# Two kinds of stores put later in the SP queue of a Fourier filter and squared-ReLU network

## The chip, the cores and the metric

The kernel runs on one core of a Trainium2 chip. A core has a matrix engine (TensorE, "PE" in the profile), VectorE ("DVE"), ScalarE ("ACT"), GpSimd ("POOL") and SyncE ("SP"), which here only issues transfers. Each engine takes its own instructions in program order and waits on semaphores for the others. Sixteen DMA engines move the data of all queues. The metric is the device time of one launch in microseconds (us); lower is better.

## The reference

`x` has 8 batches of 3008 positions by 256 features. Each feature is filtered in the frequency domain along the positions; the result goes, row by row, through a network with a squared ReLU.

```python
X = np.fft.rfft(x, axis=1)                       # x: (8, 3008, 256)
y = np.fft.irfft(X * (filt_r + 1j * filt_i)[None], n=3008, axis=1)
h = np.maximum(y.reshape(24064, 256) @ w_in, 0)  # w_in: (256, 2048)
out = (h * h) @ w_out                            # w_out: (2048, 256)
```

Inputs and the output are float32.

## The kernel before, in words

**The transform.** 3008 is 64 times 47, and the filter is done as four rounds of small matrix products, in float16, with two trips through memory to turn the layout. For batch `b`:

- `load_x` (L186, on GpSimd's queue) brings a piece of `x` in, `unit_a` (L333, four for a batch) does the 47-point part. ScalarE (L354, L362) and VectorE (L356) copy the sums from `psA` to a tile `u`, of which there are three, and `write_u` (L326, called at the end of `unit_a`, L363) stores it with two transfers on SP's queue to `dU` in memory.
- `read_u` (L403) brings the whole batch back from `dU` in the other layout (`ut`, one buffer), with two transfers, 1.5 MB together. `unit_b` (L410, twelve a batch) does the 64-point part and multiplies by the filter on VectorE (L424); GpSimd's queue adds two halves (L431). `unit_p` (L454, twelve) goes back; ScalarE copies (L463) to `ze`, and after each third `unit_p` SP stores a block to `dZ` (L466). These are the four blocks `dZ`(b,0) to `dZ`(b,3).
- `read_z` (L475, four a batch, two transfers each, at L479) brings `dZ` back as `zt`, in one of two buffers. Every `read_z` reads from the results of all four blocks. `unit_y` (L483, sixteen) does the last part: PE at L497, copies at L504 and L506 to `yt`, the network's input.

**The network.** It runs in 47 groups of 512 rows. The main loop (L805) goes through slots, eight for each group. In slot `s`, `ffn_g1` (L511) computes two of sixteen blocks of the hidden layer into `psH`, of which there are two buffers; ScalarE applies the ReLU (L531), VectorE squares (L538). The second product of the group before runs in the same slots. Groups 0 to 45 do it with seven block products in place of eight (`products`, L629): VectorE builds sums of blocks (`sums`), PE multiplies (L640), and the output is put together in two tiles, `top` and `bot`, from three output buffers (`p_out`, L148). For group `g`, ScalarE starts `top` (L647) in slot 8g+9 and `bot` (L652) in slot 8g+13; `bot` is complete in slot 8g+15 (L657) and stored at once (L658); `top` is complete in slot 8g+16 (L661, on VectorE) and stored at once (L662). `store` (L561) uses one transfer (L578) or two or three pieces (L580), since rows are kept in a permuted order. The last group, 46, uses the plain product (L547) and `ffn_out` (L550), which stores tiles named `ost`.

**The order.** The transform of batch `b` is spread by hand over the slots before its rows are wanted. `fft_plan` (L666) gives every unit a time in slots, finds a free half slot near it, and puts the moves (`load_x`, `read_u`, `read_z`) at fixed half slots. The loop calls `run(work, s, 0)` after the first product of a slot and `run(work, s, 1)` after the second. So the order of all instructions of each engine is written out by this loop, SP's transfers too: SP takes them in that order and waits, at each, for what it needs.

Of the kernel before, what the change touches and what calls it, by code (L numbers as in the profile page):

```python
# [20 lines left out]
SLOTS = 8  # L21
# [89 lines left out]
def kernel(  # L111
# [214 lines left out]
    def write_u(b, c):  # L326
        u = us.pop((b, c))
        v = dU[b].rearrange("(m q) d -> q m d", q=48)
        for j in range(2):
            m = 16 * c + 8 * j  # L330
            nc.sync.dma_start(out=v[:, m:m + 8, :], in_=u[64 * j:64 * j + 48])

    def unit_a(b, c):  # L333

        pool, tag = (p_y, "yt") if (b, c) == (1, 3) else (p_u, "u")
        u = us[(b, c)] = pool.tile([112, 8, D], F16, tag=tag, name=f"u_{b}_{c}")
        ph = psH(f"psA_{b}_{c}")
        if b == 1 and c % 2:
            ps = [psO(f"psA_{b}_{c}_{h}").rearrange("p a d -> p (a d)") for h in range(2)]
        else:  # L340
            ps = [psF(f"psA_{b}_{c}_{h}") for h in range(2)]
        for i in range(2):
            for j in range(2):
                m = slice(4 * j + 2 * i, 4 * j + 2 * i + 2)
                for h in range(2):
                    p = slice(64 * h, 64 * h + N2)
                    o = ps[h] if i == 0 else ph[:, h, :]
                    nc.tensor.matmul(o[64 * j:64 * j + 64, :], sSA[p], x16s[(b, c)][p, m, :],  # L348
                                     start=True, stop=True)
        for h in range(2):  # L350
            o = u[:, h:h + 3:2, :]
            pv = ps[h][0:112, :].rearrange("p (e d) -> p e d", d=D)
            if h == 0 or b == 1:
                nc.scalar.copy(out=o, in_=pv)  # L354
            else:
                nc.vector.tensor_copy(out=o, in_=pv)  # L356
        o = u[:, 4:8, :].rearrange("p (e h) d -> p h e d", h=2)
        pv = ph[0:112].rearrange("p h (e d) -> p h e d", d=D)
        if b == 1:
            nc.vector.tensor_copy(out=o, in_=pv)  # L360
        else:
            nc.scalar.copy(out=o, in_=pv)  # L362
        write_u(b, c)  # L363

    def chunk_a0(c):

# [166 lines left out]
    def ffn_sq(g, s):  # L533
        n = 1 if g == NG - 1 else 2
        if (s + 1) % n:
            return
        v = h2s[g][:, 2 * (s + 1 - n):2 * s + 2, :]
        nc.vector.tensor_mul(out=v, in0=v, in1=v)  # L538
# [87 lines left out]
             ((6, 8, 16), (5, 8, 14)), ((5, 14, 16), (7, 0, 16)), ((2, 12, 16), (4, 0, 8)),  # L626
             ((4, 8, 16), (3, 0, 4)), ((3, 4, 16),))

    def products(g, k):  # L629

        f = sg[g]
        for p, m0, m1 in PARTS[k]:
            if p == 1 and m0 == 0:
                f["x"] = psO(f"psX_{g}").rearrange("p a (t c) -> p a t c", t=2)
            if p == 2 and m0 == 0:
                f["y"] = psO(f"psY_{g}").rearrange("p a (t c) -> p a t c", t=2)
            o = f["x"][:, 0] if p in (1, 6, 7, 4) else f["y"][:, 0 if p == 2 else 1]
            for m in range(m0, m1):
                q, t = divmod(m, 2)
                nc.tensor.matmul(o[:, t, :], f[p][:, q, 128 * t:128 * t + 128], sg["w"][p][:, q, :],  # L640
                                 start=(m == 0 and p in (1, 2)), stop=(q == 7),
                                 skip_group_check=True)
            if m1 < 16:
                continue
            if p == 1:
                f["top"] = p_out.tile([128, 2, 256], F32, tag="ost", name=f"top_{g}")
                nc.scalar.copy(out=f["top"][:, :, 0:128], in_=o)  # L647
            elif p == 6:
                nc.scalar.copy(out=f["top"][:, :, 128:256], in_=o)
            elif p == 7:  # L650
                f["bot"] = p_out.tile([128, 2, 256], F32, tag="ost", name=f"bot_{g}")
                nc.scalar.copy(out=f["bot"][:, :, 128:256], in_=o)  # L652
            elif p == 2:
                for v, i in ((f["top"][:, :, 0:128], 0), (f["bot"][:, :, 128:256], 1)):
                    nc.vector.tensor_add(out=v, in0=f["y"][:, i], in1=v)  # L655
            elif p == 4:
                nc.scalar.copy(out=f["bot"][:, :, 0:128], in_=o)  # L657
                store(g, 2, 2, f["bot"])  # L658
            elif p == 3:
                v = f["top"][:, :, 128:256]  # L660
                nc.vector.tensor_add(out=v, in0=o, in1=v)  # L661
                store(g, 0, 2, f["top"])  # L662

    YN = (45, 45.5, 46, 46.5, 48, 49.5, 51, 52.5, 54, 56, 58, 60, 63, 66, 69, 72)

    def fft_plan():  # L666

        fixed, units, moves = [], [], []
        for b in range(1, B):
            f = (b * S // TG) * SLOTS - (48 if b > 1 else 40)  # L670
            d = 0
            if b == 1:
                for n in range(4, 16):
                    fixed.append(((n if n < 8 else n + 2 if n < 12 else 2 * n - 7) + n % 2 / 2,
                                  unit_y, 0, n))
                moves.append((7.5, read_z, 0, 3))
                moves.append((0, read_u, b))
                d = 7
            else:
                for a in range(16):  # L680
                    if a % 2 == 0 and b > 2:
                        moves.append((f + ((-57 + 2.3 * a) if b == 3 else (-66 + 2.75 * a)),
                                      load_x, b, a // 2))
                    if a % 4 == 3:
                        units.append((f + ((-13, -9, -5.5, -3)[a // 4], -46 + 2.1 * a, -56 + 2.75 * a)[min(b, 4) - 2],
                                      unit_a, b, a // 4))
                moves.append((f + (2 if b == 2 else -6.5), read_u, b))
            for p in range(12):
                r = 12 + 16.5 * p / 11 if b == 1 else 6 + 28 * p / 11 if b == 2 else -2 + 36 * p / 11
                units.append((f + r, unit_b, b, p))  # L690
                if b == 1 and 2 <= p < 10:
                    moves.append((f + r, load_x, 2, p - 2))
                units.append((f + r + (4.5 if b == 1 else 7 - 2.5 * p / 11), unit_p, b, p))
            for c in range(4):
                moves.append((f + (40 + d / 14, 43, 48, 54)[c] - d, read_z, b, c))
            for n in range(16):
                (fixed if n < 4 else units).append((f + YN[n] - d, unit_y, b, n))
        work, used, done = {}, set(), {}
        for r, *u in fixed:
            h = int(2 * r)  # L700
            used.add(h)
            work.setdefault(h, []).append(u)
        rank = (unit_a, unit_b, unit_p, unit_y)
        for r, *u in sorted(units, key=lambda u: (rank.index(u[1]), u[0])):
            after = done.get((u[0], u[1]), -1)
            if u[0] is unit_a:
                h = min((h for h in range(max(2 * int(r) - 2, after + 1), 2 * int(r) + 12)
                         if h % 2 == 0 and not used & {h - 1, h, h + 1}),
                        key=lambda h: abs(h - 2 * r))
                used |= {h - 1, h, h + 1}  # L710
                done[(u[0], u[1])] = h
                work.setdefault(h, []).append(u)
                continue
            early = 1 if u[0] is unit_b else 3
            h = min((h for h in range(max(int(2 * r) - early, after + 1), int(2 * r) + 12)
                     if h not in used),
                    key=lambda h: (sum(h + i in used for i in (-2, -1, 1, 2)) > 2) * 2
                    + abs(h - int(2 * r)))
            used.add(h)
            done[(u[0], u[1])] = h  # L720
            work.setdefault(h, []).append(u)
        for r, *u in moves:
            work.setdefault(int(2 * r), []).append(u)
        return work
# [14 lines left out]
    for k in range(2):  # L739
        c = slice(12 * k, 12 * k + 12)  # L740
# [64 lines left out]
    for s in range((NG + 1) * SLOTS):  # L805
        g, k = divmod(s, SLOTS)
        if g < NG:
            ffn_g1(g, k)
        run(work, s, 0)
        if 8 <= s < 12:  # L810
            make_t(s - 8)
        if (s - 1) // SLOTS - 1 in SEVEN:
            products((s - 1) // SLOTS - 1, (s - 1) % SLOTS)
        if g > 0 and g - 1 not in SEVEN:
            ffn_g2(g - 1, k)
        run(work, s, 1)
        if g > 0 and g - 1 not in SEVEN:
            ffn_out(g - 1, k)
        if g - 1 in SEVEN:
            sums(g - 1, k)  # L820
        if g < NG:
            ffn_sq(g, k)


# [28 lines left out]
```

## Time and profile before

| | |
|---|---|
| time, median of 4 runs | 759.8 us (758.79 to 761.32) |
| the profiled execution | 759.58 us, its span 757.5 us |
| PE busy | 741.7 us, 98% of the span |
| VectorE busy | 656.0 us, 87% |
| ScalarE busy | 564.4 us, 75% |
| GpSimd busy | 193.7 us, 26% |
| moved by DMA | 106.51 MB, 141 GB/s in the mean |
| granted PE clock | 0.997 of full speed |

Busy time is what the engine spent in its instructions; for a wait, the profile names the engine or transfer whose semaphore came last, and it reads "who line <- whom line: us in total, times, longest". A row of a timeline begins with the start and the duration in us, then the engine, the line, the operation, the tiles (out<-in), their shapes and how often; in brackets the engine's idle time before it and who ended that. On SP's timeline ("SPq") the duration is the time to issue, not to move the data. In the chain of work that ended last, each row is a piece of that chain, with start and duration; for a transfer this is the time from issue to landing. The main loop's slots begin at about 50 us; what comes before is the transform of batch 0 and the loading of constants.

### The profile page before, as it was taken

How to read it: one execution, taken by the hardware profiler on the slowest of the kernel's cores; microseconds unless marked ns; L12 is line 12 of the kernel's file. 1: busy time of each engine (PE TensorE's matmuls, PEld its weight loads, DVE VectorE, ACT ScalarE, POOL GpSimd, SP SyncE). 2: the span in 40 equal slices, each digit the busy share in tenths (PEclk: the TensorE clock that was granted, in tenths of full speed). 3: DMA queues.
4: the chain of work that ended last, by engine and by line, in shares of the span. 5: the costliest groups of instructions: out<-in, count | busy, mean ns of one | idle time of the engine just before them, and what ended most of it. 6: DMA issues, size and time to landing. Idle time of an engine off the chain costs nothing.

```text
span 757.5 us, 20002 instructions
## 1 busy us (share of the span) xinstructions
PE 741.7 (98%) x8419; PEld 542.4 (72%) x8419; DVE 656.0 (87%) x730; ACT 564.4 (75%) x803; POOL 193.7 (26%) x267
## 2 busy tenths in 40 slices
PE   8988999999999999999999999999999999999998
PEld 6745766776777777877778776787768777777776
DVE  5859997899899998999979999899989989888783
ACT  3966787787877777787777877777787777777773
POOL 3811750244222321233203224033311222000000
PEclk9999999999999999999999999999999999999999
DMA  9986897765776466756585646774547333321011
GB/s 366 303 180 179 146 183 199 189 120 115 161 207 140 94 129 160 199 105 131 109 212 131 133 102 124 203 150 101 121 119 188 87 76 93 99 85 42 30 58 56
DMA packets 103026, 106.51 MB, mean 141 GB/s; under 512 B 10144, under 2 KB 93472, under 8 KB 101400
## 3 DMA queue, kind: packets, MB, share of 16 engines
q1 hardware_dynamic: 83496, 81.99, 35.7%
q0 software_dynamic: 19296, 23.05, 21.9%
q8 instruction: 66, 1.08, 0.6%
q10 hardware_dynamic: 144, 0.18, 0.1%
q14 instruction: 24, 0.20, 0.1%
HBM read 57.97 MB, written 48.23 MB: 140 GB/s over the span
## 4 chain that ended last, share of the span: by engine, by line
PE 88%; DVE 5%; DMA 4%; ACT 2%; issue 1%; SPq 0%; DVEq 0%; ACTq 0%
PE psH L527 40%; PE psX L640 20%; PE psY L640 16%; PE psY L497 3%; PE psB L416 3%; PE psP L461 2%; DMA f<-in_filt_i_dram 2%; PE psA L348 2%; DVE prod L424 1%; ACT h L531 1%; PE psO L547 1%; DVE h L538 1%; DMA dU<-u 1%; PE psf L284 1%; PE psf L287 1%
## 5 line engine op out<-in xcount | busy, mean ns | idle before, releaser
L531 ACT ACTIVATE h<-psH 128x1024 f16<-128x1024 f32 x376 | 384.9, 1025 | 161.6 <-PE psH L527 160.6
L527 PE MATMUL psH<-yt,sWin 128*128 128x512 f16 (+7 forms) x1728 | 386.8, 351 | 1.2 <-ACT h L531 0.4
L538 DVE TENSOR_TENSOR h<-h 128x2048 f16<-128x2048 f16 (+1 forms) x192 | 229.8, 1198 | 45.5 <-ACT h L531 45.1
L431 POOL DMA_DIRECT2D prod<-prod x168 | 138.7, 967 | 429.7 <-DVE prod L424 427.3
L527 PEld LDWEIGHTS <-sWin 128*128 128x128 f16 x1728 | 149.0, 98 | 90.5 <-issue 3.0
L640 PEld LDWEIGHTS <-sum 128*128 128x128 f16 x2944 | 181.3, 98 | 26.2 <-issue 6.3
L640 PEld LDWEIGHTS <-h 128*128 128x128 f16 x2208 | 135.6, 98 | 24.5 <-issue 5.3
L424 DVE TENSOR_TENSOR prod<-psB,sF 128x1024 f16<-128x1024 f32 x84 | 102.3, 1219 | 11.9 <-PE psB L416 11.8
L640 PE MATMUL psX<-sT,sum 128*128 128x128 f16 x1472 | 104.7, 219 | 0.0
L640 PE MATMUL psY<-sT,sum 128*128 128x128 f16 x736 | 71.2, 219 | 0.0
L640 PE MATMUL psY<-sWout,sum 128*128 128x128 f16 x736 | 56.0, 219 | 1.4 <-DVE bot L655 1.4
L616 DVE TENSOR_TENSOR sum<-sum,h 128x2048 f16<-128x2048 f16 x46 | 56.2, 1221 | 0.8
L640 PE MATMUL psY<-sWout,h 128*128 128x128 f16 x736 | 56.2, 219 | 0.0
L640 PE MATMUL psX<-sT,h 128*128 128x128 f16 x736 | 56.1, 219 | 0.0
L622 DVE TENSOR_TENSOR sum<-h,sum 128x2048 f16<-128x2048 f16 x46 | 56.0, 1217 | 0.0
L619 DVE TENSOR_TENSOR sum<-h 128x2048 f16<-128x2048 f16 x46 | 56.0, 1217 | 0.0
L613 DVE TENSOR_TENSOR sum<-h 128x2048 f16<-128x2048 f16 x46 | 55.9, 1216 | 0.0
L195 POOL DMA_DIRECT2D x<-in_x_dram x64 | 55.8, 1045 | 0.5 <-PE psA L348 0.5
L463 ACT CAST ze<-psP 128x512 f16<-128x512 f32 x84 | 49.2, 586 | 1.2 <-PE psP L461 1.1
L640 PE MATMUL psX<-sWout,h 128*128 128x128 f16 x736 | 48.7, 219 | 0.0
L506 DVE CAST yt<-psY 128x376 f16<-128x376 f32 x62 | 33.7, 543 | 14.1 <-PE psY L497 13.9
L497 PE MATMUL psY<-sC,zt 112*128 112x94 f16 x512 | 42.3, 204 | 2.2 <-DMA zt<-dZ 1.8
(78 smaller groups left out, 571.5 us busy)
## 6 DMA issues: line engine op xcount, KB each, us to landing
zt<-dZ SPq DMA_DIRECT2D x64, 192.0 KB
dU<-u SPq DMA_DIRECT2D x56, 192.0 KB
prod<-prod POOLq DMA_DIRECT2D x168, 64.0 KB, 2.9
dZ<-ze SPq DMA_DIRECT2D x28, 384.0 KB
x<-in_x_dram POOLq DMA_DIRECT2D x48, 192.0 KB, 5.3
ut<-dU SPq DMA_DIRECT2D x7, 1024.0 KB
out_dram<-bot SPq DMA_DIRECT2D x32, 128.0 KB
out_dram<-top SPq DMA_DIRECT2D x16, 256.0 KB
```

The lines of the kernel that those rows point to most:

```text
L195: nc.gpsimd.dma_start(out=t[64 * h + p0:64 * h + p1], in_=v[p0:p1, 8 * c:8 * c + 8, :])
L424: nc.vector.tensor_mul(out=prod, in0=ps.rearrange("p (a d) -> p a d", d=D).unsqueeze(1).to_broadcast([128, 2, 2, D]), in1=sF[:, :, 2 * p:2 ...
L431: nc.gpsimd.dma_start(out=prod[64 * i:64 * i + 64, 0], in_=prod[64 - 64 * i:128 - 64 * i, 1], accum_op=mybir.AluOpType.add)
L497: nc.tensor.matmul(ps[:, 94 * jj:94 * jj + 94], zt[:, 4 * (g % 2) + jj, dt * 128:(dt + 1) * 128], sSY, start=True, stop=True)
L527: nc.tensor.matmul(ps[:, i, o:o + n], sWin[:, dt, jt * 128:(jt + 1) * 128], yts[b][:, dt, r:r + n], start=(dt == 0), stop=(dt == 1))
L531: nc.scalar.activation(out=h2[:, 2 * s:2 * s + 2, :], in_=ps, func=AF.Relu)
L538: nc.vector.tensor_mul(out=v, in0=v, in1=v)
L613: nc.vector.tensor_add(out=t, in0=a21, in1=a22)
L616: nc.vector.tensor_sub(out=t, in0=f[5], in1=a11)
L619: nc.vector.tensor_sub(out=t, in0=a11, in1=a21)
L622: nc.vector.tensor_sub(out=t, in0=a12, in1=f[6])
L640: nc.tensor.matmul(o[:, t, :], f[p][:, q, 128 * t:128 * t + 128], sg["w"][p][:, q, :], start=(m == 0 and p in (1, 2)), stop=(q == 7), skip ...
```

## The change

The write of `u` leaves `unit_a` for batches 2 to 7 and is put by the planner as a move of its own, two slots after the slot of its unit (the unit stands at half slot `h`, the write at slot `h / 2 + 2`, behind what else stands in that half slot). Batch 1, whose units run before the main loop, keeps its place.

The stores of `top` and `bot` go into a list with a due slot, the slot of their completion plus one, and the loop issues those that are due at the very end of a slot. Nothing else moves, and no instruction is added or taken away.

```diff
             nc.scalar.copy(out=o, in_=pv)
-        write_u(b, c)
+        if b == 1:
+            write_u(b, c)
...
+    stores = []
+
-    def products(g, k):
+    def products(g, k, s):
...
             elif p == 4:
                 nc.scalar.copy(out=f["bot"][:, :, 0:128], in_=o)
-                store(g, 2, 2, f["bot"])
+                stores.append((s + 1, g, 2, f["bot"]))
             elif p == 3:
                 v = f["top"][:, :, 128:256]
                 nc.vector.tensor_add(out=v, in0=o, in1=v)
-                store(g, 0, 2, f["top"])
+                stores.append((s + 1, g, 0, f["top"]))
...
                 done[(u[0], u[1])] = h
                 work.setdefault(h, []).append(u)
+                moves.append((h / 2 + 2, write_u, *u[1:]))
                 continue
...
         if (s - 1) // SLOTS - 1 in SEVEN:
-            products((s - 1) // SLOTS - 1, (s - 1) % SLOTS)
+            products((s - 1) // SLOTS - 1, (s - 1) % SLOTS, s)
...
         if g < NG:
             ffn_sq(g, k)
+        while stores and stores[0][0] <= s:
+            _, i, n, ost = stores.pop(0)
+            store(i, n, 2, ost)
```

## The prediction, made before the changed kernel was run

> **What bounds the kernel now.** I first asked in which stretches TensorE (PE) is not full, since only there can an order of transfers be worth anything. The table of busy time by stretch (the span, then busy us of PE, weight loads, VectorE, ScalarE, GpSimd, then granted clock, share of the DMA engines, GB/s):
>
> ```profile
> 0.00:50.00 50.00, 43.77 (x451) 31.43 (x452) 35.12 (x44) 31.71 (x43) 25.68 (x43) 0.97 0.90 295
> 50.00:110.00 60.00, 56.22 (x561) 37.36 (x561) 53.94 (x59) 44.78 (x65) 25.71 (x35) 1.00 0.86 173
> 110.00:130.00 20.00, 18.37 (x210) 12.18 (x208) 14.52 (x18) 15.88 (x24) 0.59 (x2) 1.00 0.81 198
> 130.00:170.00 40.00, 39.43 (x479) 28.91 (x478) 37.49 (x41) 30.46 (x44) 11.51 (x15) 1.00 0.66 155
> 190.00:750.00 560.00, 559.97 (x6476) 415.06 (x6474) 496.51 (x551) 424.65 (x605) 122.57 (x163) 1.00 0.52 122
> ```
>
> From 190 to 750 PE is busy for 559.97 of 560 us at the full clock: there the change can only cost. PE lacks 3.78 us in 50 to 110, 1.63 in 110 to 130, 0.57 in 130 to 170. The list of waits of PE after 50 us says what they are:
>
> ```profile
> PE psY L497 <- DMA zt<-dZ: 1.8, 2, 1.5
> PE psY L640 <- DVE bot L655: 1.4, 3, 0.8
> PE psB L416 <- DVE prod L424: 0.9, 1, 0.9
> ```
>
> One alone is a transfer's: the first `unit_y` of batch 1 waits for `zt`. The timeline of PE gives its place, 122.75 to 124.29. The chain that ended last leads back from it through the SP queue:
>
> ```profile
> 110.12 1.03 ACT u L362
> ...
> 111.17 6.25 DMA dU<-u
> ...
> 117.48 3.88 DMA dZ<-ze
> 121.36 0.02 issue
> 121.38 2.77 DMA zt<-dZ
> ```
>
> And SP's own timeline, where x2 and x3 are the transfers of one step:
>
> ```profile
> 111.17 1.40 SPq L331 DMA_DIRECT2D dU<-u  x2
> 112.66 2.73 SPq L580 DMA_DIRECT2D out_dram<-bot  x3
> 115.50 1.29 SPq L580 DMA_DIRECT2D out_dram<-top  x3
> 117.48 0.39 SPq L466 DMA_DIRECT2D dZ<-ze  x1
> 118.02 3.67 SPq L479 DMA_DIRECT2D zt<-dZ  x2
> ```
>
> The last block of `ze` (batch 1) is evacuated by ScalarE at 113.60 to 114.22, but its write to `dZ` goes out at 117.48: ahead of it SP serves a u write, the three pieces of `bot` 2, and `top` 2, which VectorE completes only at 112.24 and SP reaches at 115.50. Then the write waits for its completion counter: SP's transfers take eight semaphores in turn, and the ninth, this one, shares the u write's, landed at 117.42. The second half of the `zt` read waits for the `dZ` landing (121.36), and PE for the read's (124.15).
>
> **What the change moves.** SP is not tied to slots: it takes its list in order, and a step put later starts later only if it comes behind another SP step. So I wrote out both orders from the planner. 24 u writes (48 transfers) and 92 stores (212 pieces by the page) get a new place, but only 8 of the writes and 22 of the stores pass anything; 36 pairs of steps swap. No instruction is added or removed, and no engine other than SP changes its order. GpSimd's queue is not passed, though its x loads share the DMA engines.
>
> *Around the stall.* Old: u(2,1), `bot` 2, `top` 2, `dZ`(1,3), `zt`(1,0), u(2,2), `zt`(1,1), u(2,3). New: `bot` 2, `dZ`(1,3), u(2,1), `zt`(1,0), `top` 2, `zt`(1,1), u(2,2), u(2,3). Worked out:
> - `bot` 2 is complete at 111.42 (ScalarE L657), so SP issues it at 111.45; by the pace of the old group of five (0.30, 1.05, 0.51 us for its first three) until about 113.4.
> - `dZ`(1,3) goes out when `ze` is done, 114.25, and not 117.48: 3.2 us earlier. Its counter was used eight transfers before by a piece of `top` 1, landed long ago.
> - Its landing. From 110 to 114 the packets of the trace are nearly all the GpSimd queue's x loads of batch 3 (587 KB, against 12 KB of SP's), so the bytes that SP issued lie waiting until 115. In the old run the first 384 KB (u) were landed by 117.96, 640 KB (with `bot`) by 118.59. In the new order 640 KB end with `dZ`: I take **118.6**. From the shortest latency of a late `dZ` write (2.76) it would be 117.0; from the longest (5.55, at 98.1) 119.8.
> - The second half of `zt`(1,0) is issued at 118.65. Old latency 2.77, with other reads of `zt` 3.7 to 3.9, and u(2,1) (384 KB) now lies ahead of it: 121.4 to 122.5, against 122.6 where PE no longer waits (it started 0.14 after the landing). So the stall of 1.54 us goes, with 0.1 to 1.2 us to spare; at the far end (119.8 + 3.9 = 123.7) 1.1 us of it stays.
>
> Here a rule of the Trainium skill can be weighed. "DMA: Bandwidth & Descriptors", in "Queues, rings and completion order", says that a DMA engine takes turns between its queues packet by packet. By the trace SP had 12 KB against 587 KB in those 4 us, nothing like equal turns. By the rule SP would have had about half of the 148 to 160 GB/s there, some 300 KB: `bot` would be gone when `dZ` comes, `dZ` would land near 117 and the margin be 2 us: the same sum, and less for the first rival below. I go by the row.
>
> *What is late next.* With PE 1.54 us earlier, slot 39's psH at 123.75 needs a buffer that ScalarE freed at 121.27. `zt`(1,1) goes out at about 120.3 behind `top` 2 (was 122.77), lands near 124.5, wanted at 128.4. `zt`(1,2) and the `ut` of batch 2 (132.15 before) also come 2 to 3 us earlier, since only `bot` 3 and not `top` 3 stands ahead; `unit_b` wants the latter at 137.7. VectorE waits again for PE at 138.60 (1.24 us idle before it), so the later waits on it (0.6 us after 124) keep their size. I allow 0.1 for waits that come back.
>
> *The u writes by themselves.* The same page, under "Rules for kernel authors", says to issue a transfer early and wait late, which speaks against this half of the change. At 1.84 us a slot (psH of slots 39 to 375: 619.1 us over 336) two slots are 3.7 us if something waits for the landing. Nothing does: u(2,3) is evacuated at 122.67 and would go out near 122.7 instead of 124.86, as the reads ahead of it are earlier too; in later batches the last u write stands six slots before its `read_u`. A u buffer (three of them) is wanted again three units later, over 8 slots in the closest case. By the rule the sum would be 3.7 higher, by the rows nothing is added; I take 0.
>
> *The stores from batch 2 on.* `bot` 8, 14, 20, 26, 32, 38 now stand behind the first `zt` read of a batch, which waits for a `dZ` landing; `top` 8, 14, 20, 26, 32 behind `read_u` (1.5 MB, landing up to 8.4 us after issue). Who waits for a store? The copy that takes its output buffer, one of three. Semaphores in the trace say that `bot` g+1 (L652) waits for `bot` g's store and `top` g+2 for `top` g's; the tail shows the same, the copy named here waiting for `bot` (landed 750.95) and not for `top` (751.63):
>
> ```profile
> 751.06 0.37 ACT L558 COPY ost<-psO 128x256 f32<-128x256 f32 x1 [1.95 <-DMA out_dram<-bot]
> ```
>
> `bot` 8: the read ahead of it is released at 206.8, so it goes out by 207.8 and lands by about 212; wanted at 215.28. `top` 8 lands near 218; its buffer is wanted by `top` 10 at 223.17. Cost 0, from cover of 3 us and more; with the cover gone, see the third rival.
>
> *The tail.* `top` 45 comes behind the first `ost` store: ready at 747.54, out at about 749.6, landed by 753.1 with its old latency of 3.52; its buffer serves the last copy at 754.02. Cost 0.
>
> **Sum.** The profiled execution took 759.58 us (span 757.5 and 2.08 around it). 759.58 - 1.54 + 0.1 = 758.14; the median of the runs stands 0.22 higher, so **758.4**. The other runs lie at 758.79 to 761.32; what a measurement tells from no change is some 0.2%, or 1.5 us, just what I forecast.
>
> **Rivals.**
> 1. *The stall is only shortened.* The x loads hold back `dZ` whatever its place in SP's order (for: the 12 KB; against: they end by 116), so the read lands near 123.7: gain 0.4, **759.4**. That nothing changes belongs here: were `zt` bound by `ze` itself, the order wouldn't matter; against it, 3.26 us between evacuation and issue.
> 2. *A wait on VectorE takes the stall's place.* It was full in 90 to 110 (18.93 of 20). Against it: it sat idle 2.34 us in front of the very step after the stall. Gain about 0.8: **759.0**.
> 3. *Slower: output buffers.* A store behind `zt` and `ut` in the rings could land too late for the next `bot`. The last piece of `bot` 8 goes out at about 208.6, so it decides if that takes over 6.7 us (its like took 1.4 to 6.5, but reads behind `ut` 8.3). At 8.3 ScalarE stands for 1.6 us in each of six batches; two psH buffers let it spread that over two slots with some 0.5 us of idle each, so about 0.6 reaches PE each time: 758.4 + 3.6 = **762.0**.
>
> **Chances and range.** The stall gone: 0.68 (own range 757.6 to 759.1, from what stays of 1.54 and the spread of a median). Rivals 1 and 2: 0.2. Rival 3: 0.12. Faster by over 0.2% (under 758.28): a little under half of the first case and few of the second, 0.40; slower (over 761.3): 0.12; the rest 0.48. The range from 757.6 to 760.6 leaves out the third rival and a tenth of the first.
>
> **What would show it.** Right: PE's wait at L497 for `zt` near 122 gone; `dZ`(1,3) out at 114.3, before u; `top` 2 after the `zt` read; waits of ScalarE at L647 and L652 for a store absent. Wrong: a `zt` landing after 122.6; a new wait of ScalarE on `out_dram`, or PE below full after 190.

## The result and the profile after

The changed kernel takes 758.21 us (median of 41 runs, 756.8 to 760.63) against 759.73 us for the kernel before, run beside it. The ratio is 0.9979, with a 95% interval of 0.9974 to 0.9985: 0.21% faster, about 1.6 us (1.1 to 2.0).

Its profiled execution took 760.63 us, the longest of the 41, with a span of 758.9 us. The same kernel was profiled a second time among the experiments (758.42 us, span 756.6 us); what only one of the two shows is not put down to the change. Line numbers are a little higher here than in the kernel before (L498 for L497, L643 for L640). First the waits of PE after 50 us in the first of them:

```profile
PE psY L498 <- DMA zt<-dZ: 2.1, 2, 1.8
PE psY L643 <- DVE bot L658: 1.4, 3, 0.8
PE psX L643 <- DMA sWout<-in_moe_w_out_dram: 1.4, 1, 1.4
```

and in the second:

```profile
PE psY L498 <- DMA zt<-dZ: 1.9, 2, 1.3
PE psY L643 <- DVE bot L658: 1.4, 3, 0.8
```

The wait for `sWout` (1.4 us, before 63 us) is for a load that stands ahead of everything the change moves, and the second profile lacks it: a stray, and it can account for 1.4 of the 2.4 us by which this execution lies over the median. But the wait for `zt` is still in the list, as long as before. Its place has changed. On the timeline of PE around 122 us (changed kernel, second profile) `psY` follows the matmuls of `psH` with no wait.

```profile
121.13 1.03 PE L528 MATMUL psH<-yt,sWin 128*128 128x512 f16 x4
121.99 0.33 PE L498 MATMUL psY<-sC,zt 112*128 112x94 f16 x4
```

The same line later, in the kernel before without a wait:

```profile
578.78 0.33 PE L497 MATMUL psY<-sC,zt 112*128 112x94 f16 x4
```

and in the changed kernel, first profile and then second:

```profile
580.20 0.33 PE L498 MATMUL psY<-sC,zt 112*128 112x94 f16 x4 [1.80 <-DMA zt<-dZ]
```

```profile
577.98 0.33 PE L498 MATMUL psY<-sC,zt 112*128 112x94 f16 x4 [1.32 <-DMA zt<-dZ]
```

So one wait of 1.54 us went (batch 1, the first read of `zt`), and one of 1.3 to 1.8 us came (batch 6, the second read). The busy time by stretch, second profile, says it as a sum: PE now has 19.91 us in 110 to 130 (18.37 before), but 558.65 in 190 to 750 (559.97 before).

```profile
110.00:130.00 20.00, 19.91 (x241) 13.91 (x240) 16.18 (x20) 17.03 (x27) 0.00 (x0) 1.00 0.83 215
130.00:170.00 40.00, 39.43 (x473) 28.77 (x471) 37.53 (x41) 30.44 (x44) 12.18 (x17) 1.00 0.65 148
190.00:750.00 560.00, 558.65 (x6463) 414.46 (x6462) 494.37 (x548) 423.08 (x601) 121.23 (x162) 1.00 0.51 121
```

**Where it was won.** SP's timeline at the first place, second profile:

```profile
110.85 1.43 SPq L581 DMA_DIRECT2D out_dram<-bot  x3
113.66 0.38 SPq L467 DMA_DIRECT2D dZ<-ze  x1
114.14 1.65 SPq L331 DMA_DIRECT2D dU<-u  x2
115.88 1.69 SPq L480 DMA_DIRECT2D zt<-dZ  x2
117.66 1.18 SPq L581 DMA_DIRECT2D out_dram<-top  x3
```

ScalarE ends `ze` at 113.63, and `dZ`(1,3) goes out at 113.66; before, it went out 3.26 us after its data. It lands at 117.07 and the read at 121.03, 0.96 us before PE comes.

**Where it was lost.** SP's timeline around batch 6, the kernel before:

```profile
563.16 0.38 SPq L466 DMA_DIRECT2D dZ<-ze  x1
564.69 0.40 SPq L578 DMA_DIRECT2D out_dram<-bot  x1
565.18 1.14 SPq L479 DMA_DIRECT2D zt<-dZ  x2
566.41 1.32 SPq L580 DMA_DIRECT2D out_dram<-top  x3
567.83 0.86 SPq L407 DMA_DIRECT2D ut<-dU  x2
568.73 0.89 SPq L479 DMA_DIRECT2D zt<-dZ  x2
```

and the changed kernel, second profile:

```profile
560.87 0.39 SPq L467 DMA_DIRECT2D dZ<-ze  x1
561.36 3.08 SPq L480 DMA_DIRECT2D zt<-dZ  x2
564.55 0.39 SPq L579 DMA_DIRECT2D out_dram<-bot  x1
565.11 0.88 SPq L408 DMA_DIRECT2D ut<-dU  x2
566.03 1.41 SPq L581 DMA_DIRECT2D out_dram<-top  x3
567.49 7.50 SPq L480 DMA_DIRECT2D zt<-dZ  x4
```

In both, the second `zt` read of batch 6 stands behind `read_u` of batch 7, 1.5 MB. The change lays two more things in its way. `bot` 32 used to go out while SP had to wait for the `dZ` landing anyway; now it goes out behind that wait. And the three pieces of `top` 32 stand between `ut` and the read, where they stood ahead of `ut`. Counted from the issue of `dZ`, the read's second half goes out 7.46 us later (6.04 before) and, by the counters of completion in the trace, lands 16.98 us later (14.82 before). Before, it landed 0.81 us ahead of PE. The landings show where the time goes: `ut` is complete 13.34 us after the issue of `dZ`, about as before (13.50); the last piece of `top` 32, which had landed by 7.36 us before, now lands after `ut`, at 15.51, and the read after that. In the first profile `ut` itself also took longer, to 15.53. How much of the loss belongs to `bot` and how much to `top` was not tested apart. In batches 2 to 5 the same swaps leave 2 us and more, as PE wants that read about 9 us after the first one; in batch 6, where no `unit_a` is left to take slots, it is wanted after 5.8 us.

### The profile page after: what moved, and what is told of

It reads as the page before. It is cut to its first block, busy times and chain, and to the rows that moved or that the text cites. A ratio compares the mean times of both kernels' runs of the same rounds, so it can differ in the third digit from the quotient of the medians.

```text
span 758.9 us, 20010 instructions
## 1 busy us (share of the span) xinstructions
PE 741.0 (98%) x8419; PEld 542.2 (71%) x8419; DVE 656.1 (86%) x730; ACT 564.5 (74%) x803; POOL 193.7 (26%) x267
## 4 chain that ended last, share of the span: by engine, by line
PE 86%; DMA 6%; DVE 5%; ACT 1%; issue 1%; SPq 1%; POOL 0%; DVEq 0%
PE psH L528 39%; PE psX L643 20%; PE psY L643 16%; PE psB L417 2%; PE psY L498 2%; PE psP L462 2%; DMA f<-in_filt_i_dram 2%; DMA sWout<-in_moe_w_out_dram 2%; PE psA L348 2%; DMA zt<-dZ 2%; DVE prod L425 1%; DVE h L539 1%; PE psO L548 1%; PE psf L284 1%; PE psf L287 1%
## 5 line engine op out<-in xcount | busy, mean ns | idle before, releaser
L643 PEld LDWEIGHTS <-sum 128*128 128x128 f16 x2944 | 181.4, 98 | 26.2 <-issue 6.3
L643 PEld LDWEIGHTS <-h 128*128 128x128 f16 x2208 | 135.6, 98 | 25.9 <-issue 6.8
L643 PE MATMUL psX<-sT,sum 128*128 128x128 f16 x1472 | 104.7, 219 | 0.0
L643 PE MATMUL psY<-sT,sum 128*128 128x128 f16 x736 | 71.2, 219 | 0.0
L643 PE MATMUL psY<-sWout,sum 128*128 128x128 f16 x736 | 56.0, 219 | 1.4 <-DVE bot L658 1.4
L643 PE MATMUL psY<-sWout,h 128*128 128x128 f16 x736 | 56.2, 219 | 0.0
L643 PE MATMUL psX<-sT,h 128*128 128x128 f16 x736 | 56.1, 219 | 0.0
L643 PE MATMUL psX<-sWout,h 128*128 128x128 f16 x736 | 48.8, 219 | 1.4 <-DMA sWout<-in_moe_w_out_dram 1.4
L498 PE MATMUL psY<-sC,zt 112*128 112x94 f16 x512 | 42.3, 204 | 2.7 <-DMA zt<-dZ 2.3
```

What stands on the lines that cost most here:

```text
L498: nc.tensor.matmul(ps[:, 94 * jj:94 * jj + 94], zt[:, 4 * (g % 2) + jj, dt * 128:(dt + 1) * 128], sSY, start=True, stop=True)
```

## The experiments

All ratios are to the kernel before on the same chip, with 95% intervals.

**The two halves alone.** First only the u writes, then only the stores:

```diff
-                stores.append((s + 1, g, 2, f["bot"]))
+                store(g, 2, 2, f["bot"])
-                stores.append((s + 1, g, 0, f["top"]))
+                store(g, 0, 2, f["top"])
```

> Only the u writes of batches 2 to 7 go two slots later; the stores keep their place. Theory (the gain is the removed wait of PE for the first zt of batch 1): dZ(1,3) now stands behind bot 2 and top 2 but ahead of u(2,1), goes out near 115.0 and lands near 119.2, so the zt read lands near 122.5: the wait of 1.54 us shrinks to 0 to 0.3, time 1.2 to 1.5 us under before. Rival (the stores that no longer block SP are what counts): wait about as before, gain under 0.4 us.

```diff
-        if b == 1:
-            write_u(b, c)
+        write_u(b, c)
-                moves.append((h / 2 + 2, write_u, *u[1:]))
```

> Only the stores of top and bot go one slot later; the u writes keep their place. Theory: dZ(1,3) passes top 2, goes out near 115.4 with u(2,1) and bot 2 ahead of it (896 KB in all), lands near 119.6, zt lands 122.4 to 123.0: the wait shrinks to 0 to 0.5 us, gain 1.0 to 1.5 us. Either half is then enough, and the two gains do not add. Rival (the two halves add up): each gives about 0.75 us.

The u writes alone: 758.36 us, ratio 0.9977 (0.9968 to 0.9986). The stores alone: 758.58 us, 0.9986 (0.9976 to 0.9996). PE's wait near 124, u writes alone and then stores alone:

```profile
124.17 0.33 PE L498 MATMUL psY<-sC,zt 112*128 112x94 f16 x4 [1.14 <-DMA zt<-dZ]
```

```profile
124.18 0.33 PE L497 MATMUL psY<-sC,zt 112*128 112x94 f16 x4 [0.48 <-DMA zt<-dZ]
```

With the u writes alone 1.14 us of the wait is left in that profile, where 0 to 0.3 was expected; with the stores alone 0.48 is left, inside the 0 to 0.5 expected. Neither half ends the wait, so "either half is enough" falls for the profiles. The times of the two do not settle how the gains add up, their intervals being wide; the profiled wait is that of one execution. What the pair of profiles does show is which half brings the loss: with the u writes alone PE has no wait at 578 us, with the stores alone there is one of 0.29.

**The early and the late part.** The new order only for the stores of groups 0 to 3 and the u writes of batch 2, and only for all the others:

```diff
-        if b == 1:
+        if b == 1 or not b < 3: 
             write_u(b, c)
...
-                stores.append((s + 1, g, 2, f["bot"]))
+                if g < 4: 
+                    stores.append((s + 1, g, 2, f["bot"]))
+                else:
+                    store(g, 2, 2, f["bot"])
...
-                moves.append((h / 2 + 2, write_u, *u[1:]))
+                if u[1] < 3:
+                    moves.append((h / 2 + 2, write_u, *u[1:]))
```

(and the same for `top`). The late part has the opposite conditions: `b > 2`, `g > 3`, `u[1] > 2`.

> The new order only up to the stores of group 3 and the u writes of batch 2; everything later as before. Theory: the whole gain is in the first 130 us, so the ratio is that of the whole change, 0.998 or a little better, and the second zt read of batch 6 keeps its margin of about 0.8 us. Rival (the later part brings something too): less than half of the gain.

> The new order only from the stores of group 4 and the u writes of batch 3 on; before that as before. Theory: the wait near 122 stays at 1.5 us and there is no gain; where the second zt read of batch 6 lands after its unit_y (as in the profile of the changed kernel, 1.80 us) the time is up to 1.7 us over before, else the same. Rival: a gain of 0.5 us and more.

The early part alone takes 757.78 us, 0.9971 (0.9962 to 0.9981): all of the gain (2.2 us, 1.4 to 2.9). The late part alone takes 760.31 us, 1.0004 (0.9996 to 1.0012): none. PE's waits for `zt` after 100 us, the late part alone:

```profile
PE psY L498 <- DMA zt<-dZ: 2.3, 2, 2.1
```

The 2.1 is the old wait near 122; the rest, 0.24 us, is at 580. In the early part alone the list after 100 us has no wait for `zt`. Both came out as expected.

**The same two places in every profile.** PE wants the first `zt` read of batch 1 between 8.4 and 8.5 us after ScalarE ends `ze`, whatever the kernel. Counted from there, the read lands after 9.90, 9.94 and 10.48 us in the three profiles with the old order (the kernel before, with and without its `zt` read moved as below, and the late part alone), after 9.53 with the u writes alone, 8.87 with the stores alone, and after 7.39 to 8.29 us in the six profiles with the whole new order there. At the second read of batch 6, the four profiles in which the stores keep their place there and the read is not moved have it land 0.64 to 0.94 us ahead of PE; in the four with the stores later PE waits 0.24 to 1.80 us. No profile of these stands against either reading.

**The changed kernel again, and the read moved out of the way.** The second `zt` read of batches 2 to 7 is put ahead of `read_u`:

```diff
-                moves.append((f + (40 + d / 14, 43, 48, 54)[c] - d, read_z, b, c))
+                moves.append((f + (40 + d / 14, 43 if b == 1 else 40.5, 48, 54)[c] - d, read_z, b, c))
```

> The changed kernel again, for a second profile and beside the next ones on the same chip. Theory: no wait near 122, ratio 0.998; a wait at the second zt read of batch 6 that is there in some executions (0 to 1.8 us) and not in the others. Rival (that wait is in every execution): 1.5 us and more of it in this profile too.

> The changed kernel, with the second zt read of batches 2 to 7 put ahead of read_u of the next batch. Theory (the 1.5 MB of ut in front of it make it late in batch 6): its margin in batch 6 grows from nothing to over 4 us, no wait for zt is left after 130 us, and the time falls by what that wait costs in the mean, 0.2 to 0.8 us under the changed kernel (ratio to before 0.997). Rival (the wait in that profile was a stray): no difference to the changed kernel.

The changed kernel: 758.12 us, 0.9985 (0.9978 to 0.9993). With the read moved: 757.29 us, 0.9971 (0.9962 to 0.9980), 0.83 us less on the same chip; the two intervals just touch. In its profile the read lands 7.02 us ahead of PE, and this is the whole list of PE's waits from 130 us on:

```profile
PE psY L643 <- DVE bot L658: 0.6, 2, 0.3
```

So the wait in batch 6 belongs to the new order. It costs the changed kernel something like 0.8 us in the mean, if all of that difference is this wait. It varies: 1.80 and 1.32 us in two profiles of the changed kernel, 0.29 and 0.24 where only the stores or only the late part have the new order.

**Who made `dZ` late in the kernel before?** SP's order is left as it was, and GpSimd's first loads of x for batch 3 are held until the first `zt` has landed:

```diff
+    def hold_x():
+        nc.gpsimd.tensor_copy(out=tiny, in_=zts[(1, 0)][0:1, 0, 0:1])
...
-                        moves.append((f + ((-57 + 2.3 * a) if b == 3 else (-66 + 2.75 * a)),
+                        moves.append((f + (max(-57 + 2.3 * a, -53.5) if b == 3 else (-66 + 2.75 * a)),
...
+                if b == 1 and c == 1:
+                    moves.append((34, hold_x))
```

> The kernel before, with SP's order untouched, but GpSimd's loads of the first x pieces of batch 3 held back until the first zt of batch 1 has landed. Theory that these loads starve SP's transfers from 110 to 115 us: u(2,1), bot 2 and top 2 land 2 us earlier, dZ(1,3) goes out by 116.5 to 117 and lands in 3 us, zt lands by 122.5 to 123: the wait falls from 1.54 to 0 to 0.4 us without the change, unless the held loads make the second zt read late in turn. Rival (SP's order alone makes it late): the wait stays over 1.0 us.

SP's timeline of this kernel:

```profile
111.06 0.82 SPq L331 DMA_DIRECT2D dU<-u  x2
111.97 2.15 SPq L580 DMA_DIRECT2D out_dram<-bot  x3
114.22 1.18 SPq L580 DMA_DIRECT2D out_dram<-top  x3
115.49 0.39 SPq L466 DMA_DIRECT2D dZ<-ze  x1
115.99 2.96 SPq L479 DMA_DIRECT2D zt<-dZ  x2
```

With u, `bot` and `top` all still ahead of it, `dZ` goes out 2 us earlier (115.49), since u(2,1) has landed at 113.71 and 114.99 (117.42 and 117.96 before) and its counter is free. The read lands at 121.47 and the wait near 122 is gone. So the rival "SP's order alone" falls: the wait took both, the order and the x loads that stood in the DMA engines, and in the profiles removing either ends it. The expectation's caveat about the held loads came true too, and they cost more than was gained. They go out at 120.57 and now hold back the second `zt` read (latency 8.16 and 8.49 us, before 3.9 and 3.8):

```profile
130.58 0.33 PE L497 MATMUL psY<-sC,zt 112*128 112x94 f16 x4 [2.24 <-DMA zt<-dZ]
```

760.85 us, 1.0028 (1.0017 to 1.0039): the wait has been moved, and the kernel is slower than before.

**Four slots in place of one.** The prediction's slower rival, output buffers that a late store keeps, with a larger dose:

```diff
-                stores.append((s + 1, g, 2, f["bot"]))
+                stores.append((s + 4, g, 2, f["bot"]))
```

(and the same for `top`).

> The changed kernel with the stores four slots late in place of one. Output buffers by the prediction's reading: bot of the next group waits for the bot store of this one, now wanted about two slots after its place; it costs only where the store stands behind a read, and ScalarE shows waits at L650 to L655 for out_dram there: 1 to 5 us slower than the changed kernel. Rival (SP runs ahead anyway, buffers never bind): the same time within 0.5 us.

783.29 us, 1.0309 (1.0287 to 1.0330), some 25 us over the changed kernel where 1 to 5 were expected. The two longest waits of ScalarE, and PE's longest:

```profile
ACT h L532 <- PE psH L528: 156.8, 320, 1.9
ACT bot L655 <- DMA out_dram<-bot: 19.8, 6, 4.4
```

```profile
PE psX L643 <- ACT bot L655: 17.1, 7, 3.7
```

`bot` of a group waits for the `bot` store of the group before, as read from the semaphores, and PE stands with it. SP's timeline ahead of one such wait (`bot` at 223.07, after 2.89 us of idle time of ScalarE):

```profile
211.99 0.85 SPq L408 DMA_DIRECT2D ut<-dU  x2
212.90 0.89 SPq L480 DMA_DIRECT2D zt<-dZ  x2
213.89 1.31 SPq L581 DMA_DIRECT2D out_dram<-bot  x3
```

The last piece of this store goes out at 214.78 and lands at 222.89. In six of the seven places the store stands like this behind `ut`, most with a `zt` read between, and its last piece takes 6.8 to 8.3 us to land; in the seventh, near 175, it stands behind a `dZ` for which SP waits. So the mechanism is the rival's, with the landing time that it named (8.3). What was too small is the price of a place: 1.5 to 3.7 us of PE in place of 0.6. The waits are not the whole loss either. Against the profile before, the span is 22.1 us longer; PE is idle for 16.4 us more and busy for 5.7 us more (747.4 us), at a granted clock of 0.99 in the mean and 0.91 from 170 to 190 us. With one slot, ScalarE has no wait for a store but, in the second profile, the one in the tail, which was there before.

**The early part, with the read moved.** The early part of the change with the order of before after it and the second `zt` read moved; the kernel before with only that read moved; and the changed kernel with it, again:

> The new order up to group 3 and batch 2 as in the early part alone, the order of before after that, and the second zt read of batches 2 to 7 ahead of the next read_u. Theory: the early part brings 2 us, and the order of before left the second zt read of batch 6 a margin of 0.6 to 0.8 us, which is held in most executions: as the early part alone, ratio 0.997, with less spread between executions. Rival (that read is late in part of the executions of before too): 0.9955 to 0.9965.

> The kernel before with that one read moved, nothing else. Theory: it was in time in before (margin 0.8 us), so at most 0.3 us is gained; ratio 0.9995 to 1.0. Rival: it was late in part of the executions, gain 0.5 us and more.

> The changed kernel with that one read moved, again, beside the two others: as in its first runs, 757.3 us and ratio 0.997; the two forms with the read moved differ by no more than 0.3 us, since the other late swaps cost nothing.

Measured, in this order: 756.78 us, 0.9969 (0.9958 to 0.9979); 759.26 us, 1.0003 (0.9995 to 1.0011); 757.43 us, 0.9973 (0.9965 to 0.9981). The read moved by itself brings nothing, since in the kernel before it was in time. With the early part it gives the lowest ratio of the study, 2.25 us under the kernel before on its chip; from the early part alone (0.9971), where the read is in time too, it can't be told apart. The two forms with the read moved differ by 0.65 us, more than the 0.3 expected; their intervals overlap, so whether the other late swaps cost a little is open.

## Why the prediction was right, and where it was not

The forecast was 758.4 us with 0.48 for no difference beyond 0.2% and 0.40 for faster; 758.21 us and 0.21% is in the range and just past that line, with an interval (0.15 to 0.26%) that lies on both sides of it. The number is near for a reason that the prediction did not have: it left out a cost and may have been low on the gain.

- *The order of SP is all that counts, and few steps pass anything*: right. Nothing that runs on another engine changed its place, and both places where PE gained or lost are swaps in the list of 36.
- *Around the stall*: right, step by step. `dZ`(1,3) out at once when `ze` is done (predicted 0.03 us after, measured 0.03), landing after 3.42 us (4.35 taken), the second half of the read in 3.93 us (2.77 to 3.9), spare time 0.96 us (0.1 to 1.2). In the first profile the spare time was 0.56 and PE had no wait either. Rivals 1 and 2 did not show: no part of this wait is left in either profile, and PE's later waits on VectorE keep their size (0.6 us after 130).
- *The size of the gain, 1.44 us*: it was the wait of one profiled execution. The three profiles with the old order there show 1.54, 1.51 and 2.09 us, and the early part alone gained 2.2 us (1.4 to 2.9). 1.44 is at the edge of that; the mean wait may well be longer than the first profiled one, but the interval holds all three, so this is not settled.
- *Cause of the lateness*: the prediction named SP's order and let the x loads be what limits the cure (first rival). By the run with the loads held they were as much a condition of it as the order: without them the old order was in time.
- *The stores from batch 2 on, cost 0*: here the step failed. It asked who waits for a store that comes later, found the output buffers and their spare time, and that was right. It did not ask who stands behind the store. `top` 32, put behind `ut`, stands ahead of the second `zt` read of batch 6, and `bot` 32 no longer hides in SP's wait for `dZ`. Before, that read had 0.81 us to spare; the prediction measured such spare time for batch 1 alone. "There the change can only cost", of the stretch from 190 on, was the right warning and was not followed up; one of its own signs of being wrong, PE below full after 190, came true (558.65 and 558.17 of 560 us). The price is about 0.8 us by the two runs side by side.
- *Third rival, slower through output buffers*: not at one slot; real at four, with the mechanism as told and a larger price.
- *Rules weighed*: the rule on taking turns would have put the `dZ` landing near 117 in the time of the old profile, and the row 118.6. Counted from its issue it took 3.42 us in the second profile, between the 2.75 and the 4.35 of the two, and 3.90 in the first; the stretch itself went by the row again, with 3.5 KB for SP against 648 KB from 110 to 114 us of the second profile. The rule to issue transfers early was rightly given no price for the u writes: alone they made the kernel faster.

## What to carry to other kernels

A transfer put later in an in-order queue gives time to everything that it used to block, and takes it from everything that it now stands in front of: list both for each swap, with the spare time of each reader in every period of the loop, the last ones too, where the work thins out and the wants come closer together. A large load in that queue makes the places right behind it the worst in the list; small reads that are wanted soon belong in front of it. And a wait found in one profile is one draw: before its size goes into a sum, a second profile tells how far it varies.

## What the runs showed of the hardware

Three things were not expected. For 4 us (110 to 114, kernel before) GpSimd's x loads left SP's transfers almost no bytes (12 KB against 587 KB). With the loads held SP moved 432 KB in the same 4 us, and its u write landed 3 to 3.7 us earlier. Yet when the held loads went out later, the two queues moved about equal shares from 122 to 124 us (190 KB for SP, 192 KB for GpSimd), so equal turns describe the second stretch and not the first. Why the first was so lopsided is open.

The latency of a small read went by what was issued ahead of it: 192 KB of `zt` took about 3 to 4 us with little ahead of it, and 8 to 10 us right behind 1.5 MB of `ut`. The held x loads, of another queue, made it 8 us too.

And SP took about 0.4 us to issue one transfer (the median), but at times much longer: 1.65 us for the single piece of `top` 3 near 129.6 in the first profile of the changed kernel, and 2.34 us for the longest u write of the kernel before. What makes such an issue long was not tested. Steps that only stand in line there have a price too.
